# A fused attention + MoE + Sinkhorn-MoE kernel on one core: gate matmuls in column quarters, one reciprocal per set of items, two elementwise steps moved to ScalarE, and weight loads moved in the DMA order

## The chip, the cores and the metric

The kernel runs on one core of a Trainium2 chip. Its engines have an instruction queue each and work through it in order: TensorE (PE in the profile; its weight loads are PEld), VectorE (DVE), ScalarE (ACT), GpSimd (POOL) and SyncE (SP), which issues most of the DMAs. The metric is device time in microseconds of one execution. TensorE's clock has two levels, 1.2 and 2.4 GHz; the profile's PEclk is the mean granted clock of a stretch, 1.00 being 2.4 GHz.

## The reference

```python
# attention: B=4 batches, H=8 heads, S=576 positions, D=64
bias  = -(cum[:, :, :, None] - cum[:, :, None, :])       # cum = cumsum(max(s, 0))
scores = where(causal, -1e9, q @ k.T / 8 + min(bias, 0))
attn  = exp(scores - scores.max(-1)); attn /= attn.sum(-1) + 1e-9
x = (attn @ v) as (2304, 512)
# MoE1: w_in (512, 2048), w_out (2048, 512)
h = x @ w_in;  g = where(h > 0, h, exp(min(h, 0)) - 1);  x = g @ w_out
# MoE2: w_gate (512, 8), w1 (8, 512, 1024), w2 (8, 1024, 512)
P = exp(x @ w_gate - max)
for _ in range(8):
    P /= P.sum(1) + 1e-9;  P /= P.sum(0) + 1e-9;  P *= 2304 / 8
out = sum over e of P[:, e] * (max(x @ w1[e], 0) @ w2[e])
```

All in float32.

## The kernel before, in words

**Order.** The program is written by a small planner: `flow.pe(cost, fn)` writes a piece of TensorE work and advances a model clock, and `flow.after(dt, fn)` writes the work behind it (evictions, softmax steps) once that clock has gone on by dt. The framework then sets the order of each engine's queue; an engine takes its queue strictly in that order.

**Attention.** A job is a pair of heads of one batch; an item is 64 query rows of a job. Batch 0 is cut in two chunks ("A", keys up to 256, four items a job; "B", the other five items), batches 1 to 3 are whole chunks ("F"), four jobs each. Items go in sets (`SETS`), whose scores are made together by `qk_set` (L302). For each item GpSimd makes the bias tile R (`r_step`, L273 and L276); VectorE adds the scores and takes the row's extreme (L321, into `sm`); ScalarE takes the exponential with its row sum (L329, followed by a read of the accumulator); VectorE adds 1e-9 to that sum and takes the reciprocal (L333, L334), an item at a time; GpSimd multiplies R by it (L337, `norm`). TensorE then transposes R (L364, L370), ScalarE and VectorE copy the transposes out, and `pv_piece` multiplies by V (L431). R has five buffers, and a new R waits for the transpose of an old one.

**MoE1.** Its matmuls (L677 for w_in, L709 for w_out, 12 per group) split each float32 into two fp32r parts, so a weight is decoded first: loaded by SyncE into `st` (L581, `w_dma`), then seven operations on VectorE and two on ScalarE (L614 to L634). The activation is `relu` and exp on ScalarE (L685, L686), then on VectorE a combination (L689), the rounding of the result to fp32r (L691) and the remainder (L692). The first groups run between the attention pieces, so the attention of later batches lies beside MoE1 of the earlier ones. `w_dma` is first called after the DMAs of the first attention jobs.

**Gate.** When a batch's MoE1 output `acc` is complete, `gate(b)` multiplies it by w_gate (L789): five blocks of up to 128 tokens, in each the tokens are the stationary operand and the eight columns of w_gate stream past, four 128-row steps of the model width, each float32 matmul in two instructions: 40 for a batch. VectorE copies the result to `P_t` (L797, L799).

**Sinkhorn and MoE2.** After the gate of the last batch the eight Sinkhorn rounds start (`rows` on VectorE, L833 to L837, then `cols` with a matmul with ones, L844, then L848 to L850). They are written between the MoE2 products (L1023; A, B and C in the names) and second layers (L1092, b). From about 750 us to the end MoE2 alone runs.

Of the kernel before, what the change touches and what calls it, by code (L numbers as in the profile page):

```python
# [92 lines left out]
def kernel(  # L93
# [17 lines left out]
    NX = 3  # L111

# [20 lines left out]
    for b in range(B - 1, B - 1 - NX, -1):  # L133
# [17 lines left out]
        "wg": cst.tile([P, 4, E], F32, tag="wg", name="wg"),  # L151
# [128 lines left out]
    sms = {}  # L280

    def qk_set(n):
# [22 lines left out]
        base = set_cost(n) + 0.05  # L305
        for i, c0, keys, ps in later:
            base = softmax(i, c0, keys, ps, base)

    def softmax(i, c0, n, ps, base):
# [4 lines left out]
        if i not in sms:  # L314
            sms[i] = att.tile([P, 8], F32, tag="sm", name=f"sm{i}", bufs=8)
# [10 lines left out]

        def ex():
            mn = sm[:, 2:3] if m == LAST else sm[:, 0:1]
            nc.scalar.activation(R[:, 0:keys], R[:, 0:keys], AF.Exp, scale=-1.0, bias=mn,  # L329
                                 accum_out=sm[:, 3:4])  # L330
# [5 lines left out]
        def norm():  # L336
            nc.gpsimd.tensor_scalar(out=R[:, 0:keys], in0=R[:, 0:keys], scalar1=sm[:, 5:6], scalar2=1.0,  # L337
                                    op0=ALU.mult, op1=ALU.mult)
# [3 lines left out]
        if last:  # L342
            flow.after(base + 0.2 + d, ex)
            flow.after(base + 0.55 + 2 * d, rec)
            flow.after(base + 0.75 + 2 * d, norm)
            ready["t", i] = flow.now + base + 1.15 + 3.2 * d
# [100 lines left out]
    set_chunk = []  # L447
    for j, (k, b, p, part) in enumerate(jobs):
        at = {m: job_items[j][0] + x for x, m in enumerate(spans[part])}
        seen_r = set()  # L450
        for x in SETS[part]:
# [5 lines left out]
            set_chunk.append(k)  # L457
    bundles = []
# [211 lines left out]
    def l1_group(u, k, f, w, c0, n):  # L670
        def fn():
# [29 lines left out]
    def l2_group(u, k, q, d, w, c0, n):  # L701
        def fn():
# [14 lines left out]
            def ev():  # L717
# [9 lines left out]
                if x2[b] == 8:  # L727
                    gates.append(b)
# [48 lines left out]
    def gate(b):  # L777

        x, wg_t = accs[b], phc["wg"]
        ps = ps_s.tile([P, 512], F32, tag="S", name=f"gate{b}")  # L780
        parts, t0 = [], b * S
        while t0 < (b + 1) * S:
            r0 = t0 % P
            n = min(P - r0, (b + 1) * S - t0)
            parts.append((t0 // P, r0, n, t0 - b * S))
            t0 += n
        for i, (tt, r0, n, c0) in enumerate(parts):
            for d in range(4):
                nc.tensor.matmul(ps[r0 : r0 + n, 8 * i : 8 * i + 8], x[:, d, c0 : c0 + n], wg_t[:, d, :],  # L789
                                 start=(d == 0), stop=(d == 3))  # L790
        whole = [i for i, x in enumerate(parts) if x[2] == P]
        half = next(i for i, x in enumerate(parts) if x[2] < P)

        def ev():
            L = phc["P"]
            i, tt = whole[0], parts[whole[0]][0]
            nc.vector.tensor_copy(L[:, tt : tt + 4, :], ps[:, 8 * i : 8 * i + 32].rearrange("p (t e) -> p t e", t=4))  # L797
            tt, r0, n, _ = parts[half]
            nc.vector.tensor_copy(L[r0 : r0 + n, tt, :], ps[r0 : r0 + n, 8 * half : 8 * half + 8])  # L799
            phc["logits"] = phc.get("logits", 0) + 1  # L800
        flow.after(0.2, ev)
# [29 lines left out]
    def rows():  # L831
# [6 lines left out]
        phc["step"] += 1  # L838

# [24 lines left out]
    def extras(force=False):  # L864
        while extra and (force or extra[0][0]()):
# [279 lines left out]
    nc.sync.dma_start(phc["wg"], wg)  # L1145
    nc.vector.memset(ones, 1.0)
    make_identity(nc, ident)
    nc.gpsimd.memset(mask, 0.0)
# [36 lines left out]
    w_dma()  # L1185

    def att_wait():
        t = att_next_ready()
        if t > flow.now:
            flow.flush(t)  # L1190
            flow.now = t

# [14 lines left out]
    for g in range(len(groups)):  # L1207
# [31 lines left out]
        while gates:  # L1239
            flow.pe(2.5, lambda: gate(gates.pop(0)))  # L1240
# [4 lines left out]
    while gates:  # L1245
        flow.pe(2.5, lambda: gate(gates.pop(0)))
# [53 lines left out]
```

## Time and profile before

| | |
|---|---|
| median of three runs | 2211.27 us (2206.74 to 2213.00) |
| the profiled execution | 2213.01 us, of which the span of the profile 2211.2 us |
| TensorE busy | 2151.1 us (97%), 12236 matmuls |
| VectorE, ScalarE, GpSimd busy | 59%, 43%, 37% |
| mean granted clock of TensorE | 0.983 |

The profile is of one execution, and its span leaves out 1.8 us of that execution's time. A TensorE that is busy is not at full speed: its clock may be at the lower level, and short matmuls cost more than their columns. Idle time of an engine, and what ended it, is listed per engine as a wait.

### The profile page before, as it was taken

To read this page: it belongs to the slowest core of one execution; us is meant where nothing else is said; L and a number is where in the kernel's file an instruction comes from. 1 tells how busy PE (TensorE), PEld (TensorE's weight loads), DVE (VectorE), ACT (ScalarE), POOL (GpSimd) and SP (SyncE) were. 2 spreads that over 40 slices of the span, in tenths; PEclk is the share of its full clock that TensorE was granted. 3 is DMA by queue.
4 is the path that set the end of the run, shared out by engine and by line. 5 is a ranking of instruction groups with operands and counts; after the bars stand their busy time and mean duration, and the time that the engine had idled before them with its cause. 6 is when DMAs were issued, how large, how long until landed. Compare 5 with 4: busy or idle time off the path is not lost.

```text
span 2211.2 us, 33504 instructions
## 1 busy us (share of the span) xinstructions
PE 2151.1 (97%) x12236; PEld 1901.1 (86%) x12236; DVE 1294.1 (59%) x2921; ACT 940.2 (43%) x2201; POOL 823.3 (37%) x1046
## 2 busy tenths in 40 slices
PE   6789999999999999999999999999999999999999
PEld 3357988999998898989998989989899899899898
DVE  5678698555756755555555555555555455555554
ACT  3565545343433444344434444343434443443432
POOL 5676343232402343333333343433333333434330
PEclk8899999999999999999999999999999999999999
DMA  6454444243562421222215221222115221222121
GB/s 198 154 167 169 145 169 159 79 131 106 188 229 96 150 77 59 66 77 67 67 58 195 77 77 58 67 68 76 65 60 195 77 70 56 76 67 77 58 67 38
DMA packets 102227, 228.55 MB, mean 103 GB/s; under 512 B 8816, under 2 KB 24688, under 8 KB 102064
## 3 DMA queue, kind: packets, MB, share of 16 engines
q1 hardware_dynamic: 97456, 209.65, 28.9%
q10 hardware_dynamic: 4608, 16.78, 1.9%
q8 instruction: 96, 1.57, 0.3%
q14 instruction: 67, 0.55, 0.1%
HBM read 189.10 MB, written 37.30 MB: 102 GB/s over the span
## 4 chain that ended last, share of the span: by engine, by line
PE 88%; DVE 5%; POOL 2%; DMA 1%; ACT 1%; issue 1%; SPq 0%; POOLq 0%; DVEq 0%; ACTq 0%
PE b L1092 36%; PE A L1023 18%; PE C L1023 9%; PE n L709 7%; PE m L677 7%; PE B L1023 5%; PE S L302 2%; PE X L431 2%; PE T L364 1%; PE gate L789 1%; DVE R L321 1%; POOL R L273 1%; DVE h L692 0%; DMA xr<-x_d 0%; DVE r L689 0%
## 5 line engine op out<-in xcount | busy, mean ns | idle before, releaser
L1092 PE MATMUL b<-w,h 128*128 128x512 f32 x3456 | 844.7, 393 | 0.0
L1092 PEld LDWEIGHTS b<-w,h 128*128 128x128 f32 x3456 | 645.5, 188 | 125.1
L906 POOL TENSOR_TENSOR w1c<-S,w1c 128x512 fp32r<-128x512 f32 x192 | 263.6, 1395 | 860.6 <-ACT w1c L905 860.6
L1023 PE MATMUL A<-xc,w1c 128*128 128x384 f32 x2304 | 449.5, 336 | 0.0
L1106 DVE SCALAR_TENSOR_TENSOR acc<-b,P_t,acc 128x512 f32<-128x512 f32 x264 | 197.5, 748 | 423.1 <-PE b L1092 423.1
L1023 PEld LDWEIGHTS A<-xc,w1c 128*128 128x128 f32 x2304 | 406.3, 188 | 7.8
L1036 ACT ACTIVATE h<-pre_P 128x384 fp32r<-128x384 f32 x288 | 151.4, 526 | 437.6 <-DVE pre_P L1049 437.3
L677 PE MATMUL m<-xT,w 128*128 128x288 f32 (+2 forms) x1536 | 231.3, 305 | 2.9 <-DVE r L689 1.5
L1023 PE MATMUL C<-xc,w1c 128*128 128x384 f32 x1152 | 233.9, 337 | 0.0
L709 PE MATMUL n<-h,w 128*128 128x288 f32 (+2 forms) x1536 | 222.3, 299 | 3.3 <-DVE r L689 1.6
L677 PEld LDWEIGHTS m<-xT,w 128*128 128x128 f32 x1536 | 214.2, 194 | 12.4 <-issue 5.0
L709 PEld LDWEIGHTS n<-h,w 128*128 128x128 f32 x1536 | 207.3, 188 | 17.3 <-issue 11.1
L1023 PEld LDWEIGHTS C<-xc,w1c 128*128 128x128 f32 x1152 | 206.0, 189 | 7.5
L906 DVE TENSOR_TENSOR w<-sw,w 128x512 fp32r<-128x512 f32 x192 | 155.5, 831 | 59.9 <-ACT w L905 59.9
L1039 DVE SCALAR_TENSOR_TENSOR h<-pre_P,h 128x384 fp32r<-128x384 f32 x288 | 160.8, 558 | 12.3 <-ACT h L1036 0.5
L273 POOL TENSOR_SCALAR R<-cum,cum_m 128x256 f32<-128x256 f32 (+4 forms) x144 | 101.8, 707 | 155.5 <-PE T L370 90.6
L337 POOL TENSOR_SCALAR R<-R,sm 128x64 f32<-128x64 f32 (+8 forms) x144 | 92.5, 650 | 118.6 <-DVE sm L334 64.0
L1036 ACT ACTIVATE h<-A 128x384 fp32r<-128x384 f32 x96 | 47.2, 491 | 192.8 <-PE A L1023 192.8
L905 ACT CAST w<-sw 128x512 fp32r<-128x512 f32 x192 | 109.4, 619 | 21.5 <-PE n L709 16.8
L1057 ACT COPY pre_P<-A 128x384 f32<-128x384 f32 x192 | 92.4, 481 | 60.1 <-PE A L1023 60.1
L1023 PE MATMUL B<-xc,w1c 128*128 128x384 f32 x576 | 117.5, 339 | 0.0
L1023 PEld LDWEIGHTS B<-xc,w1c 128*128 128x128 f32 x576 | 104.6, 190 | 7.8 <-issue 0.2
(162 smaller groups left out, 2288.2 us busy)
## 6 DMA issues: line engine op xcount, KB each, us to landing
sw<-in_w_dram SPq DMA_DIRECT2D x192, 512.0 KB, 3.3
w<-w_sc SPq DMA_DIRECT2D x56, 512.0 KB, 3.6
w_sc<-w ACTq DMA_DIRECT2D x32, 512.0 KB, 3.3
xc_d<-xs SPq DMA_DIRECT2D x28, 384.0 KB, 3.2
xc<-xc_d SPq DMA_DIRECT2D x14, 768.0 KB, 6.0
QK<-in_qk_dram SPq DMA_DIRECT2D x16, 576.0 KB, 5.1
st<-in_wi_dram SPq DMA_DIRECT2D x16, 512.0 KB, 4.5
st<-in_wo_dram SPq DMA_DIRECT2D x16, 512.0 KB, 4.0
```

Source lines behind the costliest of these rows:

```text
L273: nc.gpsimd.tensor_scalar(out=t[:, 0:w], in0=ct[j].rearrange("p w k -> p (w k)")[:, S * z : S * z + w], scalar1=8.0, scalar2=cum_m[:, z, m ...
L337: nc.gpsimd.tensor_scalar(out=R[:, 0:keys], in0=R[:, 0:keys], scalar1=sm[:, 5:6], scalar2=1.0, op0=ALU.mult, op1=ALU.mult)
L677: nc.tensor.matmul(ps[:, 0:n], t[:, a, d * P : (d + 1) * P], x[:, z, d, c0 : c0 + n], start=(d == 0 and o == 0), stop=(d == 3 and o == 2))
L709: nc.tensor.matmul(ps[:, 0:n], t[:, a, f * P : (f + 1) * P], h[:, z, c0 : c0 + n], start=(f == 0 and o == 0), stop=(f == 3 and o == 2))
L905: nc.scalar.copy(hi, x)
L906: eng.tensor_tensor(out=lo, in0=x, in1=f32(hi), op=ALU.subtract)
L1023: nc.tensor.matmul(ps, t[:, a, wi_, kt * P : (kt + 1) * P], x[:, z, kt], start=(first and kt == 0 and o == 0), stop=(kt == 1 and o == 2), ...
L1036: nc.scalar.activation(h[:, 0], src, AF.Relu)
L1039: nc.vector.scalar_tensor_tensor(out=h[:, 1], in0=src, scalar=0.0, in1=f32(h)[:, 0], op0=ALU.max, op1=ALU.subtract)
L1057: nc.scalar.copy(new(name), ps)
L1092: nc.tensor.matmul(ps, h[:, z, c0 : c0 + P], t[:, a, :], start=(f == 0 and o == 0), stop=(f == 3 and o == 2))
L1106: nc.vector.scalar_tensor_tensor(out=a, in0=ps, scalar=q, in1=a, op0=ALU.mult, op1=ALU.add)
```

## The change

- **Gate.** `wg` is stored 32 columns wide (24 of them zero). `gate(b, z)` takes a column part z of the batch (256 or 320 tokens): the four 128-row steps are now four matmuls with w_gate stationary and `acc` streaming, each writing its own 32 partitions of one PSUM tile. ScalarE copies the tile out (`lt`), and `gate_sum` adds the four quarters and turns the tokens to partitions, by a matmul of each block of `lt` with a selection matrix `sel`. VectorE copies the logits to `P_t` as before. The queue of gates is a list of such steps, run between MoE1 groups.
- **Softmax.** The row sums of a set stand in one tile (`sums`), and one pair of VectorE operations a set makes all their reciprocals; the multiplications of the set follow. For the chunks A and B (batch 0) they are on ScalarE, for the others on GpSimd as before.
- **MoE1.** The rounding of the activation to fp32r (L691) is on ScalarE.
- **Sinkhorn.** A column step is written no sooner than 3 us of model time after the row step.
- **DMAs.** The first two weights are requested right after the first QK, ahead of the other DMAs of the start; w_gate is requested after those.

```diff
+    SINKGAP = 3.0
+    NORM_ACT = 2
...
+    def norm(i, q):
+        R, keys = Rt[i], 64 * (items[i][1] + 1)
+        if set_chunk[place[i][0]] < NORM_ACT:
+            nc.scalar.activation(R[:, 0:keys], R[:, 0:keys], AF.Copy, scale=q)
+        else:
+            nc.gpsimd.tensor_scalar(out=R[:, 0:keys], in0=R[:, 0:keys], scalar1=q, scalar2=1.0,
+                                    op0=ALU.mult, op1=ALU.mult)
...
         def rec():
-            nc.vector.tensor_scalar(out=sm[:, 4:5], in0=sm[:, 3:4], scalar1=1e-9, scalar2=None, op0=ALU.add)
-            nc.vector.reciprocal(sm[:, 5:6], sm[:, 4:5])
+            nc.vector.tensor_scalar(out=su[:, 0:count], in0=su[:, 0:count], scalar1=1e-9, scalar2=None, op0=ALU.add)
+            nc.vector.reciprocal(su[:, 5 : 5 + count], su[:, 0:count])
+            for t in set_t[n_set]:
+                norm(t, su[:, 5 + place[t][1] : 6 + place[t][1]])
...
-                nc.vector.tensor_copy(h[:, 0, c0 : c0 + n], r[:, 0:n])
+                nc.scalar.copy(h[:, 0, c0 : c0 + n], r[:, 0:n])
...
+    def gate(b, z):
         x, wg_t = accs[b], phc["wg"]
+        cut = [0, 256 + 64 * (b % 2), S]
+        c0, n = cut[z], cut[z + 1] - cut[z]
+        lt = mo1.tile([P, 320], F32, tag="lt", name=f"lt{b}_{z}", bufs=1)
+        ps = ps_s.tile([P, 512], F32, tag="S", name=f"gate{b}_{z}")
+        for d in range(4):
+            nc.tensor.matmul(ps[32 * d : 32 * d + 32, 0:n], wg_t[:, d, :], x[:, d, c0 : c0 + n],
+                             start=True, stop=True)
+        def ev():
+            nc.scalar.copy(lt[:, 0:n], ps[:, 0:n])
+            gates.append((gate_sum, b, z, lt, c0, n))
+        flow.after(1.1, ev)
+
+    def gate_sum(b, z, lt, c0, n):
...
+        for i, (tt, r0, m, at) in enumerate(parts):
+            nc.tensor.matmul(ps[r0 : r0 + m, 8 * i : 8 * i + 8], lt[:, at : at + m], phc["sel"],
+                             start=True, stop=True)
+        if z == 0:
+            gates.append((gate, b, 1))
...
+        phc["due"] = flow.now + SINKGAP
...
-        while extra and (force or extra[0][0]()):
+        while extra and (force or (extra[0][0]() and flow.now >= phc.get("due", 0.0))):
...
     qk_load(0)
-    nc.sync.dma_start(phc["wg"], wg)
+    w_dma()
...
-    w_dma()
+    nc.sync.dma_start(phc["wg"][:, :, 0:E], wg)
+    sel = phc["sel"]
+    nc.gpsimd.tensor_tensor(out=sel, in0=ident[:, 0:E], in1=ident[:, 32 : 32 + E], op=ALU.add)
+    for i in (64, 96):
+        nc.gpsimd.tensor_tensor(out=sel, in0=sel, in1=ident[:, i : i + E], op=ALU.add)
```

The queues of the two programs show what moves. A row is one operation, output `<-` inputs, its shape and how often it stands there in a row; a float32 matmul is one row here and two instructions in the trace.

TensorE's queue from the gate of the last batch to the second transfer of the Sinkhorn's start, before:

```order
L789 MATMUL gate_8314<-wg,acc_7331 64x8 x4
L789 MATMUL gate_8314<-wg,acc_7331 128x8 x7
L1023 MATMUL A_8344<-xc_0_7154,w1c_7565 128x384 x3
L789 MATMUL gate_8314<-wg,acc_7331 128x8 x9
L1023 MATMUL A_8344<-xc_0_7154,w1c_7565 128x384 x3
L1023 MATMUL C_8355<-xc_3_7189,w1c_7565 128x384 x6
L812 MATMUL mxt<-ident,small 1x128
```

and of the change:

```order
L809 MATMUL gate_0_8203<-acc_7220,wg 32x320 x3
L1066 MATMUL A_8233<-xc_0_7041,w1c_7454 128x384
L809 MATMUL gate_0_8203<-acc_7220,wg 32x320
L1066 MATMUL A_8233<-xc_0_7041,w1c_7454 128x384 x4
L827 MATMUL gs_0_8209<-sel,lt_0_8202 64x8
L827 MATMUL gs_0_8209<-sel,lt_0_8202 128x8 x2
L809 MATMUL gate_1_8216<-acc_7220,wg 32x256 x4
L1066 MATMUL A_8233<-xc_0_7041,w1c_7454 128x384
L1066 MATMUL C_8244<-xc_3_7075,w1c_7454 128x384 x2
L827 MATMUL gs_1_8222<-sel,lt_1_8215 128x8 x2
L1066 MATMUL C_8244<-xc_3_7075,w1c_7454 128x384 x4
L854 MATMUL mxt<-ident,small 1x128
```

Twenty gate matmuls have become eight and five (`gs`); before each `gs` stand four or three product matmuls. In the gates of the other batches 24 matmuls of MoE1 stand there.

VectorE's queue at the start, before (cum_m and cum are what the first R is made of):

```order
L247 SCALAR_TENSOR_TENSOR s_raw<-ones,s_raw 32x576
L1167 COPY aB_106<-s_raw 32x9x64
L245 TENSOR_SCALAR cum_134<-cum_134 128x256
L247 SCALAR_TENSOR_TENSOR cum_134<-ones,cum_134 128x256
L1174 TENSOR_SCALAR cum_m<-cT 64x144 x2
```

and of the change (db and da belong to the decoding of the first two weights):

```order
L250 SCALAR_TENSOR_TENSOR s_raw<-ones,s_raw 32x576
L1211 COPY aB_107<-s_raw 32x9x64
L638 TENSOR_SCALAR db_196<-db_196 128x512
L639 TENSOR_SCALAR da_195<-db_196 128x512
L638 TENSOR_SCALAR db_218<-db_218 128x512
L641 SCALAR_TENSOR_TENSOR da_195<-st_114,da_195 128x512
L1218 TENSOR_SCALAR cum_m<-cT 64x144 x2
L248 TENSOR_SCALAR cum_139<-cum_139 128x256
L1221 TENSOR_SCALAR cum_m<-cT 64x144
L250 SCALAR_TENSOR_TENSOR cum_139<-ones,cum_139 128x256
```

Four decoding operations, for which both weights must have landed, now stand ahead of cum_m.

ScalarE's queue at the start, in the change (before, no multiplication stands between the exponentials):

```order
L349 ACTIVATE R_169,sums_184<-R_169,sm_183 128x64
L349 ACTIVATE R_169,sums_184<-R_169,sm_185 128x128
L349 ACTIVATE R_186,sums_207<-R_186,sm_206 128x192
L349 ACTIVATE R_186,sums_207<-R_186,sm_208 128x256
L319 ACTIVATE R_169<-R_169,sums_184 128x64
L319 ACTIVATE R_169<-R_169,sums_184 128x128
L349 ACTIVATE R_209,sums_233<-R_209,sm_232 128x64
L349 ACTIVATE R_209,sums_233<-R_209,sm_234 128x128
```

The rows of L319 are the multiplications; they wait for VectorE's reciprocals, and the next job's exponentials stand behind them.

## Rows read from the trace of the kernel before

**Rows 1.** Windows: stretch, length, busy us (count) of PE, PEld, DVE, ACT, POOL, PEclk, DMA.

```profile
0.00:125.00 125.00, 93.05 (x497) 48.93 (x498) 77.85 (x302) 56.69 (x169) 77.61 (x147) 0.84 0.55 180
125.00:200.00 75.00, 67.83 (x510) 48.04 (x511) 64.10 (x233) 48.52 (x154) 55.92 (x91) 0.98 0.54 180
...
560.00:620.00 60.00, 55.44 (x406) 54.23 (x406) 42.41 (x75) 26.86 (x65) 27.45 (x24) 0.97 0.71 236
...
685.00:750.00 65.00, 57.23 (x277) 51.12 (x276) 46.33 (x111) 26.66 (x56) 28.38 (x29) 0.87 0.42 137
750.00:2211.00 1461.00, 1457.48 (x7279) 1311.96 (x7277) 775.31 (x1290) 593.94 (x1218) 510.58 (x542) 1.00 0.23 77
```

**Rows 2.** Windows, same columns: each of the four gates and the stretch behind it.

```profile
400.50:404.80 4.30, 4.30 (x44) 4.26 (x42) 0.90 (x3) 0.85 (x2) 0.00 (x0) 0.99 0.01 4
404.80:410.00 5.20, 5.20 (x29) 5.20 (x29) 2.33 (x8) 1.08 (x3) 0.00 (x0) 0.68 0.00 0
...
439.80:445.60 5.80, 5.80 (x42) 5.77 (x41) 0.21 (x2) 0.63 (x2) 0.58 (x1) 0.72 0.00 0
445.60:450.00 4.40, 4.40 (x23) 4.40 (x23) 1.99 (x8) 1.71 (x4) 0.69 (x1) 0.60 0.05 7
...
580.80:586.00 5.20, 4.74 (x44) 4.61 (x43) 5.19 (x9) 2.98 (x7) 3.40 (x3) 0.97 0.40 146
586.00:592.00 6.00, 6.00 (x36) 6.00 (x36) 3.99 (x12) 2.97 (x7) 1.35 (x1) 0.74 0.81 269
...
685.80:692.80 7.00, 7.00 (x45) 6.96 (x44) 1.62 (x2) 0.62 (x1) 2.45 (x4) 0.66 0.77 237
692.80:700.00 7.20, 7.20 (x28) 6.55 (x28) 2.25 (x8) 1.84 (x5) 3.00 (x3) 0.62 0.00 1
```

**Rows 3.** Chain that ended last, 600 to 800 us: start, us, what.

```profile
685.89 2.22 PE gate L789 x22
...
689.21 3.64 PE gate L789 x18
```

**Rows 4.** TensorE's waits, 0 to 125 us: us in total, times, longest.

```profile
PE T L364 <- POOL R L337: 11.5, 6, 2.5
...
PE T L370 <- POOL R L337: 2.4, 1, 2.4
```

**Rows 5.** TensorE's waits, 200 to 2211 us, same columns.

```profile
PE col L844 <- DVE small L837: 7.8, 5, 2.9
...
PE n L709 <- DVE r L689: 1.6, 1, 1.6
```

**Rows 6.** TensorE timeline near 460 us: start, us, line, shapes of the first matmul.

```profile
460.59 1.07 PE L302 MATMUL S<-QK 64*64 64x512 f32 x8
```

**Rows 7.** Chain that ended last, 0 to 300 us: one job's V matmuls.

```profile
184.44 2.21 PE X L431 x20
```

**Rows 8.** Groups by line, 0 to 200 us: busy us, mean ns, then idle before.

```profile
L337 POOL TENSOR_SCALAR R<-R,sm 128x64 f32<-128x64 f32 (+8 forms) x70 | 49.0, 705 | 23.8 <-DVE sm L334 10.2 <-DVE aA L378 3.6 <-ACT r L685 2.9
L329 ACT ACTIVATE R<-R,sm 128x64 f32<-128x64 f32 (+8 forms) x71 | 39.6, 559 | 21.5 <-DVE sm L321 15.9 <-DVE sm L325 5.5
...
L618 DVE SCALAR_TENSOR_TENSOR da<-st,da 128x512 int32<-128x512 int32 x16 | 11.6, 723 | 0.0
...
L334 DVE RECIPROCAL sm<-sm 128x1 f32<-128x1 f32 x70 | 10.2, 151 | 0.1
...
L333 DVE TENSOR_SCALAR sm<-sm 128x1 f32<-128x1 f32 x70 | 9.5, 141 | 5.8 <-ACT R L329 5.4
```

**Rows 9.** Timeline of the start: the first R, and one item's two reciprocal operations.

```profile
8.84 0.85 POOL L273 TENSOR_SCALAR R<-cum,cum_m 128x128 f32<-128x128 f32 x2 [6.14 <-DVE cum_m L1174]
...
21.17 0.12 DVE L333 TENSOR_SCALAR sm<-sm 128x1 f32<-128x1 f32 x1
...
25.37 0.15 DVE L334 RECIPROCAL sm<-sm 128x1 f32<-128x1 f32 x1
```

**Rows 10.** Groups by line, VectorE, 200 to 690 us.

```profile
L691 DVE CAST h<-r 128x288 fp32r<-128x288 f32 (+2 forms) x115 | 40.2, 351 | 2.7
```

More of the change, by code (lines that the diff above doesn't have):

```diff
@@ L278, in r_step @@
         cum_advance()
-    sms = {}
+    sms, sums = {}, {}
     def qk_set(n):
@@ L305, in qk_set @@
         base = set_cost(n) + 0.05
+        later.sort(key=lambda x: place[x[0]][1] - 9 * (x[1] > 0))
         for i, c0, keys, ps in later:
             base = softmax(i, c0, keys, ps, base)
+    NORM_FIXED = 0.2
+    def norm(i, q):
[5 more added lines that the diff above has]
+                                    op0=ALU.mult, op1=ALU.mult)
     def softmax(i, c0, n, ps, base):
@@ L325, in ttr @@
                 nc.vector.tensor_tensor(out=sm[:, 2:3], in0=sm[:, 0:1], in1=sm[:, 1:2], op=ALU.min)
+        n_set, at, count = place[i]
+        if last and n_set not in sums:
+            sums[n_set] = att.tile([P, 10], F32, tag="sums", name=f"sums{n_set}", bufs=3)
+        su = sums.get(n_set)
         def ex():
@@ L343, in softmax @@
             flow.after(base + 0.2 + d, ex)
-            flow.after(base + 0.55 + 2 * d, rec)
-            flow.after(base + 0.75 + 2 * d, norm)
-            ready["t", i] = flow.now + base + 1.15 + 3.2 * d
+            if at == count - 1:
+                flow.after(base + 0.55 + 2 * d, rec)
+                when = flow.now + base + 0.95 + 2 * d
+                for t in set_t[n_set]:
+                    when += NORM_FIXED + 64 * (items[t][1] + 1) / 800.0
+                    ready["t", t] = when
         return base + 0.1 + n / 950.0
@@ L457 @@
             set_chunk.append(k)
+            for x, t in enumerate(set_t[-1]):
+                place[t] = (len(sets) - 1, x, len(set_t[-1]))
     bundles = []
@@ L727, in ev @@
                 if x2[b] == 8:
-                    gates.append(b)
+                    gates.append((gate, b, 0))
             flow.after(12 * _mm(n) + 0.05, ev)
@@ new lines, in gate_sum @@
+    def gate_sum(b, z, lt, c0, n):
+        ps = ps_s.tile([P, 512], F32, tag="S", name=f"gs{b}_{z}")
+        parts, t0 = [], b * S + c0
+        while t0 < b * S + c0 + n:
+            r0 = t0 % P
+            m = min(P - r0, b * S + c0 + n - t0)
+            parts.append((t0 // P, r0, m, t0 - b * S - c0))
+            t0 += m
+        for i, (tt, r0, m, at) in enumerate(parts):
[3 more added lines that the diff above has]
+            gates.append((gate, b, 1))
@@ L791, in gate @@
         whole = [i for i, x in enumerate(parts) if x[2] == P]
-        half = next(i for i, x in enumerate(parts) if x[2] < P)
+        half = [i for i, x in enumerate(parts) if x[2] < P]
         def ev():
             L = phc["P"]
[L796 to L800, printed above, removed]
@@ L801, in gate @@
-        flow.after(0.2, ev)
+            i, tt, k = whole[0], parts[whole[0]][0], len(whole)
+            nc.vector.tensor_copy(L[:, tt : tt + k, :],
+                                  ps[:, 8 * i : 8 * i + 8 * k].rearrange("p (t e) -> p t e", t=k))
+            for i in half:
+                tt, r0, m, _ = parts[i]
+                nc.vector.tensor_copy(L[r0 : r0 + m, tt, :], ps[r0 : r0 + m, 8 * i : 8 * i + 8])
+            phc["logits"] = phc.get("logits", 0) + z
+        flow.after(0.8, ev)
@@ L1191, in att_wait, with gates_run @@
             flow.now = t
+    def gates_run():
+        while gates:
+            fn, *args = gates.pop(0)
+            flow.pe(1.0, lambda: fn(*args))
     def att_end(k):
@@ L1238 @@
                 w1_prep(int(g > m2["w"] + 24), 0.0)
-        while gates:
-            flow.pe(2.5, lambda: gate(gates.pop(0)))
+        gates_run()
         w_advance(g)
@@ L1245 @@
     while gates:
-        flow.pe(2.5, lambda: gate(gates.pop(0)))
+        gates_run()
+        flow.drain()
     pools["xp%d" % ((B - 1) % NX)].release()
```

24 lines of the change are left out of this document (6 added, 18 removed).

## Prediction

> **What bounds the kernel now.** I read the windows by stage first, because 97% busy over the span hides where the rest lies. From 750 us to the end TensorE is busy 1457.48 of 1461 us at a clock of 1.00 [rows 1]; no edit touches that stage, so it ends as much earlier as it starts. Up to 750 us the loss is in four places: 32 us of idle time and a clock of 0.84 in the first 125 us, 7.2 us idle to 200 us, 4.6 us between 560 and 620 us, 7.8 us and a clock of 0.87 between 685 and 750 us [rows 1]. The second thing to see is that the gates are costly though TensorE is never idle in them. Each takes 4 to 6 us, and three of the four stretches right behind a gate run at a granted clock of 0.60 to 0.68, the fourth at 0.74, so most of each at 1.2 GHz; in the first gate itself it is still 0.99, at 2.4 GHz [rows 2]. Third, the waits: in the first 125 us TensorE's largest wait is for GpSimd's multiplication by the reciprocal, 11.5 and 2.4 us [rows 4]; behind 200 us it is the Sinkhorn column step that waits for VectorE, 7.8 us in five waits [rows 5].
>
> **The gates: -17 us.** Before, the four take 4.30, 5.80, 5.20 and (2.22 + 3.64) 5.86 us, together 21.2 [rows 2, 3]. The new first half streams 576 columns a batch through four quarters, two instructions each: 576 x 4 x 2 = 4608 column passes. Nothing in the trace streams through quarters of the array's columns. The nearest rows: the V matmuls use halves of the columns, and one job's 20 instructions carry 4 x 1216 = 4864 passes in 2.21 us, 0.454 ns a pass [rows 7]; the score matmuls use 64 x 64 corners, all four in turn, and the set of the 512- and 448-key pieces carries 4 x 960 = 3840 passes in 1.07 us, 0.279 ns [rows 6]. So more tiles side by side cost less per pass. At 0.279 a batch costs 1.3 us, at 0.454 it costs 2.1, and if quarters don't overlap at all, while the halves do, twice that, 4.2. I take 1.3, as four tiles are what the score matmuls have too. The second half is five matmuls a batch of the old kind (weights of 128 columns, eight columns streamed), 10 instructions at 4.30 / 40 = 0.107 us [rows 2]: 1.1 us. That is 2.4 us a batch, 9.6 in all: -11.6.
>
> The clock comes on top. Behind the gates it costs 5.2 x 0.32 + 4.4 x 0.40 + 6.0 x 0.26 + 7.2 x 0.38 = 7.7 us [rows 2]. In place of 40 short matmuls in a row stand at most 10, and full groups of MoE1 between them; I expect the three dips in MoE1 to go (5.0 us) and half of the last (1.4): -6.4.
>
> Against it, the last gate has little cover. In the queues four product matmuls stand between its first part and the `gs` that needs ScalarE's copy, three between its second part and its `gs`; the copy is bounded by ScalarE's other operations of that size, about 0.56 us [rows 8], and a queued weight rounding can stand ahead of it. I charge 1.5 us for both waits and the longer way to the Sinkhorn start (0 to 4). For the other batches 24 matmuls cover the copy. Sum -16.5, rounded to -17; bounds -20 (nothing for the waits, all dips gone) and -2 (quarters one after the other: 21.2 against 21, clock -6, wait +4).
>
> The Trainium skill, "TensorE: Matmul & The Clock Gate", section "Measured speedup vs the span model", gives 3.07 times for four packed tiles, not four. By it the 4.2 us of a batch would be an estimated 1.4 instead of 1.3, so the sum would be 0.4 us worse; no run here shows it yet.
>
> **The softmax of batch 0 and the early weights: -8 us.** GpSimd's multiplications cost it 705 ns each [rows 8], and in its queue stand new R tiles, which wait for transposes; so the multiplications wait for work they don't need. In the first two chunks 36 of them (16 + 20) go to ScalarE. Its exponentials of the same shapes cost 559 ns [rows 8], which I take as the price: 20 us more on an engine that is busy 56.7 of 125 us [rows 1], so 61%: it has room. TensorE's 13.9 us of waits [rows 4] don't all vanish, since ScalarE has its own queue (copies, exponentials, decoding): I take half, -7. The clock in that stretch costs up to 125 x 0.16 = 20 us [rows 1], but much of that lies where TensorE has nothing to do; I take -3. Against it stands the start. The first R is made at 8.84 us, when cum_m is there [rows 9]. Now cum_m stands behind four decoding operations, at most 0.72 us each [rows 8], and these behind two weight transfers. Before, no decoding stood ahead of it, so the first R comes later: +2 (0 to 3). The same decoding is then missing later, where it held a reciprocal back from 21.17 to 25.37 us [rows 9]; that is in the -7. Sum -8. Bounds: -22 (all of the waits, 10 us of clock, no delay) and +8 (the waits come back behind ScalarE's queue and the start is later).
>
> The reciprocal pair costs 151 + 141 ns [rows 8] and there are 56 pairs now for 144: VectorE loses 26 us of work. In batches 1 to 3 the first item of a set now waits for the last one's exponential, up to four more of 559 ns. TensorE has MoE1 groups meanwhile, and loses 7 us in all up to 200 us [rows 1]: I put 0, between -4 and +4.
>
> **The rounding on ScalarE: -2 us.** VectorE gives away 128 roundings of 351 ns [rows 10], 45 us. That pays only where TensorE waits for it: in the 4.6 us of idle time between 560 and 620 us, where VectorE is busy 42 of 60 us [rows 1], and in single waits such as 1.6 us [rows 5]. The path gets one more hand-over between engines, covered by the four PSUM buffers of MoE1 (`ps_m`). I take -2 (-6 to +3). What moves to ScalarE (about 50 us by the same 559 ns less the short shapes) finds it less than half busy.
>
> **The Sinkhorn: -2 us.** Between the first and the last column step TensorE's queue has 102 product and 50 second-layer matmuls before, 89 and 60 after: about the same work. So the gap of 3 us evens the spacing but adds little cover; VectorE's chain stays as it is. The last step, ahead of which stood 12 + 4 matmuls, now has 9 + 12. Of 7.8 us [rows 5] I take back 2; bounds -7.8, and +3 if the later start pushes the last step into the second layers that need it.
>
> **Sum.** 2213.0 (the execution profiled, span 2211.2 and 1.8 around it) - 17 - 8 - 2 - 2 = 2184. The median of the runs before is 1.7 below that execution, so I forecast **2182**.
>
> **Rivals.**
> *Start won whole.* If GpSimd's queue was the only brake of batch 0, TensorE's waits all go and the clock follows: -20 instead of -8, 2170. For it: GpSimd is the releaser of the largest wait [rows 4]. Against: VectorE is as busy as GpSimd there, 77.85 and 77.61 us [rows 1]. Chance 0.18.
> *Waits change their name.* ScalarE takes the multiplications in order, behind four exponentials and the copies of transposes, and the waits stay as long: start 0, so 2190. Chance 0.16.
> *Quarters don't run side by side.* Then the gates give about 5 us instead of 17: 2194. For it: no row shows quarters. Against: [rows 6] against [rows 7]. Chance 0.14.
> *ScalarE is blocked: slower.* A multiplication at the head of ScalarE's queue waits for the set's reciprocal, which waits in VectorE's queue, once for 4.2 us behind decoding [rows 9]; the next job's exponentials, the copies of transposes and the MoE1 activations stand behind it. Batch 0 has 20 sets. The other edits give 21 us; so the kernel is slower by 6.6 us from 27.6 us on, 1.4 us a set beyond what the waits before cost; at 2 us a set it ends at 2230. Against: early decoding empties VectorE's queue. Chance 0.04.
> The Trainium skill, "ScalarE: Activation LUTs", section "Rules for kernel authors", would have multiplications on VectorE and not on ScalarE: it is on this rival's side. Whether the trace agrees is open, since no row before has a plain multiplication on ScalarE.
>
> **How the numbers follow.** About 6.6 us (0.3%) is what a measurement of this kernel tells from no change. The forecast's case, 2172 to 2192, has 0.43; the first three rivals 0.48; the slow one 0.04; 0.05 is for two of the bad cases together (start at +8 and gates at -3: 2200 to 2214). Faster is all of the first two groups: 0.90; same 0.06; slower 0.04. The range takes in the 2194 of the quarters and reaches to 2201 for part of the mixed case, and below to 2164, where the start gives all and the Sinkhorn its waits; some 0.15 is left out.
>
> **What would show it.** The gates' `gate` matmuls take 0.5 to 0.8 us a part, and the clock behind them is 1.00. TensorE's waits for GpSimd in the first 125 us are gone, those for ScalarE's multiplication are below 7 us; the first R comes at 10 to 12 us. The idle time of 560 to 620 us falls below 3 us; the column steps' waits are 5 to 6 us. The stage behind them takes the same 1461 us. The prediction is wrong if the dips of the clock stay (+6), if a part of the gate takes over 1.5 us, or if batch 0's attention ends later than before.

## The result and the profile after

The changed kernel takes 2188.89 us (median of four executions, 2187.69 to 2194.79), beside 2211.26 for the kernel before: a ratio of 0.9907, 95% interval 0.9884 to 0.9931, so 20.6 us less by the ratio. The profiled execution took 2194.79 us, with a span of 2192.7, 18.2 us less than the profiled execution of before. This one and a second profiled one (2193.68 us) are slower than the other three (2187.69 to 2189.91), so a mark read from their traces can be some 5 us late.

The windows by stage, with the columns of [rows 1]:

```profile
0.00:125.00 125.00, 90.14 (x531) 49.15 (x532) 74.92 (x269) 75.77 (x223) 60.37 (x128) 0.90 0.55 181
125.00:200.00 75.00, 67.97 (x486) 48.57 (x485) 59.31 (x181) 48.67 (x151) 51.20 (x79) 0.96 0.52 179
560.00:620.00 60.00, 53.71 (x368) 49.96 (x367) 35.45 (x63) 31.91 (x81) 23.78 (x21) 0.94 0.70 232
685.00:750.00 65.00, 59.30 (x299) 52.42 (x299) 53.19 (x125) 35.20 (x74) 29.66 (x28) 0.95 0.45 150
750.00:2192.00 1442.00, 1438.99 (x7222) 1307.64 (x7221) 768.46 (x1276) 585.96 (x1201) 509.91 (x540) 1.00 0.23 77
```

The first 125 us did not get better: TensorE is idle 34.9 us there, 3 more than in [rows 1], at a better clock. The stretch from 560 to 620 us is worse (6.3 us idle for 4.6), the one from 685 to 750 better. Where the waits of [rows 4] went shows in TensorE's waits, 0 to 125 us (us in total, times, longest). Before, the score matmuls waited so:

```profile
PE S L302 <- DVE sm L321: 5.8, 4, 3.5
PE S L302 <- DMA QK<-in_qk_dram: 4.5, 1, 4.5
```

and changed:

```profile
PE S L305 <- DVE sm L336: 11.8, 7, 6.9
PE S L305 <- DMA QK<-in_qk_dram: 11.4, 2, 7.0
PE T L385 <- ACT R L319: 3.0, 3, 1.6
```

The multiplication is waited for 3.0 us now (13.9 in [rows 4]), 10.9 less. The score matmuls wait 6.0 us more for VectorE and 6.9 more for the QK transfer. From 200 us on, answering to [rows 5]:

```profile
PE col L887 <- DVE small L879: 4.5, 3, 2.2
PE n L732 <- ACT h L714: 2.7, 1, 2.7
...
PE gs L827 <- ACT lt L813: 0.4, 1, 0.4
```

The gate of batch 0 in TensorE's timeline (start, us, line, shape of the first matmul):

```profile
403.05 0.64 PE L809 MATMUL gate<-acc,wg 128*32 128x256 f32 x8
403.61 3.46 PE L700 MATMUL m<-xT,w 128*128 128x288 f32 x24
406.91 0.51 PE L827 MATMUL gs<-sel,lt 128*128 128x8 f32 x4
407.34 0.75 PE L809 MATMUL gate<-acc,wg 128*32 128x320 f32 x8
408.02 3.45 PE L700 MATMUL m<-xT,w 128*128 128x288 f32 x24
```

The next matmul starts 0.56 and 0.68 us after the two parts, 1.24 in this batch; the forecast was 1.3 by [rows 6]. In batch 2 the order cuts a part into six instructions and two, so that one quarter stands alone in the timeline:

```profile
574.25 0.62 PE L809 MATMUL gate<-acc,wg 128*32 128x256 f32 x2 [0.81 <-DVE acc L744]
574.80 1.84 PE L700 MATMUL m<-xT,w 128*128 128x288 f32 x12
```

One quarter of 256 columns takes 0.55 us to the next matmul, four take 0.56: side by side they cost what one costs, which is 3.9 times. The Trainium skill, "TensorE: Matmul & The Clock Gate", section "Measured speedup vs the span model", has 3.07 times for four tiles along the rows of the array. By that figure a batch was an estimated 1.4 us; the trace of these quarters, which lie along the columns, is better. The timeline also shows the price of cutting a part: both pieces take nearly the time of the whole, so batches 2 and 3, where a part is cut, take 1.86 and 1.89 us for their quarters.

The stretches behind the four gates, with the columns of [rows 2], now run at a clock of 1.00, where they had 0.60 to 0.74. In batch 2's gate itself (572.60 to 587.50 us), where TensorE is idle for 3 us, this execution has 0.89; in the second profiled execution the clock is 1.00 there too.

```profile
412.20:420.00 7.80, 7.80 (x62) 6.52 (x62) 5.27 (x19) 4.90 (x17) 4.12 (x10) 1.00 0.30 81
...
446.50:452.00 5.50, 5.50 (x43) 5.41 (x44) 3.34 (x11) 4.06 (x13) 0.00 (x0) 1.00 0.50 156
...
572.60:587.50 14.90, 11.90 (x78) 9.65 (x76) 11.17 (x19) 9.11 (x22) 5.50 (x6) 0.89 0.63 211
587.50:594.00 6.50, 6.50 (x50) 6.42 (x49) 4.94 (x11) 5.16 (x14) 2.62 (x3) 1.00 0.69 245
...
688.00:694.00 6.00, 6.00 (x36) 5.68 (x35) 3.17 (x7) 3.90 (x9) 3.69 (x3) 1.00 0.28 90
```

The table sets marks of TensorE's timeline side by side, for all runs (us; "end" is the start of the last second-layer matmul; the ratio is to the kernel before, timed beside it, with its 95% interval; a single execution has none). It is read down a column: what an edit gives up to the first gate, up to the last one, and to the end.

| kernel | first R | first V matmul | first gate | last gate | end | ratio |
|---|---|---|---|---|---|---|
| before | 8.84 | 21.37 | 400.65 | 685.83 | 2207.09 | |
| before, again | 8.91 | 21.43 | 400.16 | 686.73 | 2206.30 | |
| before, padded | 8.87 | 21.40 | 404.93 | 692.36 | 2203.89 | 0.9962 (0.9942 to 0.9982) |
| changed | 12.07 | 24.76 | 403.05 | 682.24 | 2188.60 | 0.9907 (0.9884 to 0.9931) |
| changed, again | 11.92 | 24.62 | 405.20 | 682.10 | 2187.47 | |
| tiles moved | 12.01 | 24.72 | 401.66 | 679.74 | 2182.90 | 0.9888 (0.9868 to 0.9908) |
| old gate | 11.98 | 24.66 | 402.67 | 686.41 | 2191.76 | 0.9946 (0.9931 to 0.9961) |
| late weights | 8.82 | 23.00 | 396.75 | 674.45 | 2179.48 | 0.9903 (0.9886 to 0.9920) |
| multiplication on GpSimd | 11.93 | 29.00 | 406.08 | 682.86 | 2187.80 | 0.9928 (0.9915 to 0.9942) |
| rounding on VectorE | 11.93 | 24.61 | 401.67 | 680.20 | 2185.12 | 0.9916 (0.9897 to 0.9935) |
| reciprocal per item | 12.04 | 25.17 | 394.22 | 670.86 | 2175.58 | 0.9848 (0.9830 to 0.9866) |
| no gap | 11.67 | 24.35 | 402.13 | 679.76 | 2187.97 | 0.9930 (0.9915 to 0.9945) |
| late weights, tiles moved | 8.90 | 22.84 | 398.89 | 676.75 | 2178.42 | 0.9883 (0.9865 to 0.9901) |
| the same, batch 1 on ScalarE | 8.80 | 22.98 | 402.28 | 680.55 | 2180.49 | 0.9881 (0.9864 to 0.9899) |

Two things stand out in the rows of before and changed. The first gate does not come earlier but 2.4 to 5.0 us *later*, and both kernels have done the same TensorE work up to there (1392 matmul instructions of MoE1, 512 of scores, 300 transposes, 336 with V). The runs "tiles moved", "old gate" and "no gap" have the changed kernel's instructions up to this mark; with them it lies between 401.66 and 405.20 us, 1.0 to 5.0 later than before. The padded kernel, with the instructions of before, has it at 404.93, so such a mark moves by 4 us without an edit, and the sign is not sure; that no 8 us were gained is. And from the start of the last gate to the end, where the prediction put some 5 us, the kernel gains 13 to 16 us.

### The profile page after: what moved, and what is told of

Same layout as the page of the kernel before. It is cut to its first block, busy times and chain, and to the rows that moved or that the text cites. A ratio compares the mean times of both kernels' runs of the same rounds, so it can differ in the third digit from the quotient of the medians.

```text
span 2192.7 us, 33164 instructions
## 1 busy us (share of the span) xinstructions
PE 2129.9 (97%) x12180; PEld 1892.3 (86%) x12180; DVE 1243.7 (57%) x2621; ACT 1000.9 (46%) x2373; POOL 804.0 (37%) x1014
## 4 chain that ended last, share of the span: by engine, by line
PE 89%; DVE 3%; DMA 3%; POOL 2%; ACT 1%; issue 1%; SPq 0%; POOLq 0%; ACTq 0%; DVEq 0%
PE b L1135 36%; PE A L1066 18%; PE C L1066 9%; PE m L700 8%; PE n L732 7%; PE B L1066 5%; PE S L305 3%; PE X L452 2%; PE T L385 1%; DMA xr<-x_d 1%; POOL R L276 1%; POOL R L279 1%; DMA xc_d<-xs 0%; DVE xc L949 0%; DMA QK<-in_qk_dram 0%
## 5 line engine op out<-in xcount | busy, mean ns | idle before, releaser
L1135 PE MATMUL b<-w,h 128*128 128x512 f32 x3456 | 831.5, 390 | 0.0
L1082 DVE SCALAR_TENSOR_TENSOR h<-pre_P,h 128x384 fp32r<-128x384 f32 x288 | 161.5, 561 | 11.6
L948 ACT CAST w1c<-S 128x512 fp32r<-128x512 f32 x192 | 110.4, 628 | 4.1 <-POOL S L981 3.8
L1100 ACT COPY pre_P<-C 128x384 f32<-128x384 f32 x96 | 46.3, 482 | 143.0 <-PE C L1066 142.8
```

Of the source, the lines that this page charges most:

```text
L948: nc.scalar.copy(hi, x)
L1082: nc.vector.scalar_tensor_tensor(out=h[:, 1], in0=src, scalar=0.0, in1=f32(h)[:, 0], op0=ALU.max, op1=ALU.subtract)
L1100: nc.scalar.copy(new(name), ps)
L1135: nc.tensor.matmul(ps, h[:, z, c0 : c0 + P], t[:, a, :], start=(f == 0 and o == 0), stop=(f == 3 and o == 2))
```

## The experiments

**Is the MoE2 stage faster by its addresses?** First both kernels once more, without an edit:

> The kernel before, profiled once more. Question: the stage of MoE2 behind the last column step became about 7 us shorter in the profile after, though no edit is in it. There two second-layer matmuls in a row start 230.6 ns apart before and 226.7 after, two product matmuls 173.7 before and 175.3 after. Theory of the addresses (the wider gate table and the new table shift the tiles that were allocated behind them by 416 bytes, and with that a matmul's pace): the same 230.6 and 173.7 again. Rival, the pace differs from execution to execution: it moves by a nanosecond or more between executions of this same kernel, towards 226.7. Time 2205 to 2214 by both.

> The changed kernel, profiled once more, as a control for the spread between executions. Theory of the addresses: second-layer matmuls start 226.7 ns apart again, product matmuls 175.3. Rival, the pace differs from execution to execution: other values. The profiled execution of 2194.79 us was the slowest of four of this kernel, so both expect a time of 2187 to 2195.

The mean spacing repeated to 0.1 ns: second-layer matmuls 230.6 ns apart in both executions of before and 226.7 in both of the changed kernel, product matmuls 173.7 and 175.3. ("Matmul" here and in the expectations is one instruction of the trace.) One turn of the repeating order in TensorE's timeline, from its first line to the same place in the next turn, before:

```profile
1001.55 2.93 PE L1092 MATMUL b<-w,h 128*128 128x512 f32 x12
...
1017.15 2.93 PE L1092 MATMUL b<-w,h 128*128 128x512 f32 x12
```

and changed:

```profile
1004.71 2.88 PE L1135 MATMUL b<-w,h 128*128 128x512 f32 x12
...
1020.23 2.88 PE L1135 MATMUL b<-w,h 128*128 128x512 f32 x12
```

The times were 2212.19 and 2193.68 us. So the pace belongs to the kernel and not to the execution. Then the addresses alone:

```diff
 "wg": cst.tile([P, 4, E], F32, tag="wg", name="wg"),
+"pad": cst.tile([P, 104], F32, tag="pad", name="pad"),
```

> The kernel before with one unused tile of 416 bytes a partition behind the gate table, so that every tile allocated behind it lies where it lies in the changed kernel; nothing else differs. Theory of the addresses: second-layer matmuls 226.7 ns apart and product matmuls 175.3, the stage behind the last column step about 7 us shorter, time 2211 - 7 = 2204 us, ratio 0.997. Rival (the pace comes from the execution, or from the time at which the stage begins, and not from addresses): 230.6 and 173.7 as before, 2211 us, ratio 1.000.

Groups by line, TensorE, 760 to 2180 us (busy us, mean ns of one): before,

```profile
L1092 PE MATMUL b<-w,h 128*128 128x512 f32 x3276 | 799.5, 393 | 0.0
L1023 PE MATMUL A<-xc,w1c 128*128 128x384 f32 x2184 | 423.6, 335 | 0.0
```

before with the pad,

```profile
L1093 PE MATMUL b<-w,h 128*128 128x512 f32 x3297 | 791.7, 389 | 0.0
L1024 PE MATMUL A<-xc,w1c 128*128 128x384 f32 x2197 | 429.5, 336 | 0.0
```

and changed:

```profile
L1135 PE MATMUL b<-w,h 128*128 128x512 f32 x3310 | 794.5, 389 | 0.0
L1066 PE MATMUL A<-xc,w1c 128*128 128x384 f32 x2186 | 427.5, 336 | 0.0
```

A tile that nothing uses gives the old kernel the new kernel's pace. From its first second-layer matmul behind the last column step to its last one it takes 1454.8 us, where before takes 1462.2: 7.4 us less, and 8.4 by the ratio. The theory of the addresses is shown; what about the address does it is not.

```diff
-"sel": cst.tile([P, E], F32, tag="sel", name="sel"),
+phc["sel"] = mo1.tile([P, E], F32, tag="sel", name="sel")
```

> The changed kernel with the table that sums the quarters (32 bytes a partition) moved from the pool of constants into that of MoE1, so that the weight and activation tiles of MoE2 lie 384 bytes (a multiple of 64) behind their place of before in place of 416; the instructions are the same. Theory that the place within 64 bytes sets the pace: second-layer matmuls 230.6 ns apart again, time 2189 + 7 = 2196 us, ratio to before 0.993. Rival (another cause): 226.7 stays, 2189 us, ratio 0.990.

The stage came out faster again, not slower (groups by line, as above):

```profile
L1135 PE MATMUL b<-w,h 128*128 128x512 f32 x3333 | 802.3, 390 | 0.0
L1066 PE MATMUL A<-xc,w1c 128*128 128x384 f32 x2178 | 422.1, 334 | 0.0
```

One turn, 36 second-layer and 42 product instructions (the later expectation, which says 12 and 24, counts wrong), takes 15.60 us before, 15.52 changed and padded, 15.48 here. So my sub-theory (the place within 64 bytes) falls: a shift by a multiple of 64 has a pace of its own.

**The gates.**

```diff
-        for d in range(4):
-            nc.tensor.matmul(ps[32 * d : 32 * d + 32, 0:n], wg_t[:, d, :], x[:, d, c0 : c0 + n],
-                             start=True, stop=True)
...
+        for i, (tt, r0, n, c0) in enumerate(parts):
+            for d in range(4):
+                nc.tensor.matmul(ps[r0 : r0 + n, 8 * i : 8 * i + 8], x[:, d, c0 : c0 + n], wg_t[:, d, 0:E],
+                                 start=(d == 0), stop=(d == 3))
```

> The changed kernel with the gate of before (40 matmuls of the row form a batch, no copy to ScalarE, no summing matmul); the tables keep their sizes, so that all tiles stay where they are. Theory of the prediction (the gates give 17 us): four gates of 4.3 to 5.9 us again, a granted clock of 0.6 to 0.75 behind each, time 2189 + 17 = 2206 us, ratio to before 0.998. Rival (what the matmul spacing of MoE2 gives, 7 us, and the other edits make up most of the gain, the gates less than half of it): 2189 + 8 = 2197 us, ratio 0.994.

The ratio lies between the two, nearer to the rival: the gates give 0.0039 of 2211 us, 8.6, half of what was forecast. Where the time goes, from 150 us to the start of the Sinkhorn (time from each matmul's start to the next one's, without idle time, summed by kind from the trace; us):

```
                        before  old gate  changed  changed, again
gate and its sum         19.94     18.84    11.35           10.95
MoE1, two layers        415.95    414.59   413.40          411.06
idle                     14.04     13.29    16.28           17.39
```

The shorter gate saves 7.5 to 7.9 us, MoE1's matmuls run 1.2 to 3.5 us faster, and TensorE is idle 3.0 to 4.1 us more. The old gate stands here for one execution; in the second one of before it sums to 17.84 us and in the padded kernel to 20.72, so the saving is known to about 2 us. At the full clock MoE1's 288-column matmuls are 132.5 ns apart with the old gate as with the new, so what they gain is the clock. By place, the gain is between the first gate and the third (175.85 us with the old gate, 169.76 and 169.70 with the new); from the last gate to the end the old gate takes 1505.35 us and the new one 1506.36 and 1505.37, so the last gate gave nothing. That idle time is in the stretch of batch 2's gate. TensorE's waits, 560 to 620 us, with the old gate:

```profile
PE gate L814 <- DVE acc L744: 2.0, 2, 1.2
PE m L700 <- DVE acc L744: 0.6, 2, 0.4
```

and changed:

```profile
PE m L700 <- DVE acc L744: 2.4, 3, 1.8
PE m L700 <- DVE r L712: 1.8, 1, 1.8
PE m L700 <- ACT acc L742: 0.8, 2, 0.7
```

MoE1 waits there for VectorE and ScalarE either way; as I read it, the long gate was work that filled part of the wait.

**The first weights.**

```diff
     qk_load(0)
-    w_dma()
...
+    w_dma()
     nc.sync.dma_start(phc["wg"][:, :, 0:E], wg)
```

> The changed kernel with the first two expert weights loaded and decoded at the place of before, behind the first set of R. Theory (the early transfers and decodings are what makes the start late: first R at 12.07 us for 8.84, second QK transfer issued at 9.88 us for 4.96): first R at 9 us again, first V matmuls at 21 us for 24.8, and about 3 us less, 2186 us, ratio 0.989. Rival (TensorE makes it up by 125 us anyway, or the decodings then hold the reciprocals back as in the kernel before): the first R at 9 us, but the first gate of batch 0 where it was (403 to 405 us), time 2189 to 2192 us, ratio 0.990 to 0.992.

The first R is back at 8.82 us, the first V matmul at 23.00. The profiled execution gains 6.3 to 8.5 us up to the first gate and keeps it to the end, more than either expected; but at 2185.55 us it is among the shortest of its six, which reach from 2185.42 to 2195.12, and the ratio says 0.9 us. So no gain of the early weights shows; that they cost something, one trace suggests and the times don't settle.

**The multiplication on ScalarE.**

```diff
-    NORM_ACT = 2
+    NORM_ACT = 0
```

> The changed kernel with all multiplications by the reciprocal on GpSimd, as before; the shared reciprocals stay. Theory of the prediction (GpSimd's queue is the brake of batch 0): TensorE waits for the multiplication 10 us or more in the first 125 us again, chunk B's last V matmuls at 119 us for 112, time 2189 + 6 = 2195 us, ratio 0.993. Rival (the waits only change their name; TensorE waited for VectorE and for transfers in the changed kernel, 23 us in the first 125): time 2187 to 2190 us, ratio 0.989 to 0.991.

TensorE's waits, 0 to 125 us:

```profile
PE T L385 <- POOL R L321: 13.7, 6, 3.3
PE S L305 <- DVE sm L336: 9.3, 8, 6.7
PE S L305 <- DMA QK<-in_qk_dram: 4.9, 2, 4.5
```

GpSimd is waited for again, and the transfer 6.5 us less: in sum TensorE is idle 35.6 us for 34.9, the last gate and the end stand where they were. That is on the rival's side (waits change their name). The marks that the theory named came, too: chunk B's last V matmuls start at 117.90 us for 112.16 and 111.55, and the median is 2195.00 us; by the ratio it is 4.6 us longer, with intervals that overlap. Executions of the changed kernel differ by 7 us among themselves (2187.69 to 2194.79), so one end in the same place decides nothing. Up to 5 us are open.

**The rounding.**

```diff
-                nc.scalar.copy(h[:, 0, c0 : c0 + n], r[:, 0:n])
+                nc.vector.tensor_copy(h[:, 0, c0 : c0 + n], r[:, 0:n])
```

> The changed kernel with the rounding of MoE1's inner values back on VectorE (a copy of up to 512 columns, 351 ns each in the profile before). Theory of the prediction (VectorE is the brake of single stretches): the idle time between 560 and 620 us stays at or above 6.3 us, TensorE waits for VectorE in more places before 685 us, time 2189 + 2 = 2191 us, ratio 0.992. Rival (neither engine is waited for there, since the idle time of that stretch did not fall with the edit: 4.6 us before, 6.3 after): time 2187 to 2190 us, the same waits; if ScalarE's extra work is what made the stretch worse, the idle time falls to 4.6 us and the time to 2187 us.

The ratio is 2.0 us above that of the changed kernel, inside its interval, and the trace ends 2.4 to 3.5 us earlier. The idle time of 560 to 620 us is 6.9 us, so neither engine's rounding made it. What the rounding is worth stays open.

**The shared reciprocals.**

```diff
-            nc.vector.reciprocal(su[:, 5 : 5 + count], su[:, 0:count])
-            for t in set_t[n_set]:
-                norm(t, su[:, 5 + place[t][1] : 6 + place[t][1]])
+            nc.vector.reciprocal(su[:, 5 + at : 6 + at], su[:, at : at + 1])
+            norm(i, su[:, 5 + at : 6 + at])
...
-            if at == count - 1:
-                flow.after(base + 0.55 + 2 * d, rec)
...
+            flow.after(base + 0.55 + 2 * d, rec)
+            ready["t", i] = flow.now + base + 1.15 + 3.2 * d
```

> The changed kernel with a reciprocal and a multiplication by itself for each score row block, as before (144 pairs of short VectorE operations for 56); the multiplications of batch 0 stay on ScalarE. Theory (the pairs cost VectorE some 26 us, and the start waits for VectorE, 11.8 us in the first 125): 2 to 4 us slower, 2191 to 2193 us, ratio 0.991 to 0.992. Rival (a set's first rows are ready earlier by up to four exponentials, which is worth as much as the pairs cost): 2187 to 2190 us, ratio 0.989 to 0.991.

Both were wrong by sign or size: 2178.14 us, 13.0 us *less* than the changed kernel by the ratio. The windows, 0 to 125 us:

```profile
0.00:125.00 125.00, 96.94 (x608) 55.36 (x609) 83.88 (x347) 84.35 (x248) 71.00 (x142) 0.97 0.56 185
```

VectorE is busy 9 us longer than in the changed kernel, and TensorE 6.8 us longer at 0.97 for 0.90. TensorE's timeline at the wait of 7 us, changed:

```profile
36.78 1.32 PE L305 MATMUL S<-QK 64*64 64x320 f32 x2 [6.98 <-DMA QK<-in_qk_dram]
38.04 1.55 PE L452 MATMUL X<-aA,V 128*64 128x256 f32 x8
```

and with a reciprocal per item:

```profile
31.57 1.76 PE L305 MATMUL S<-QK 64*64 64x192 f32 x8
...
33.69 0.87 PE L447 MATMUL X<-aA,V 128*64 128x256 f32 x8
...
35.78 1.51 PE L305 MATMUL S<-QK 64*64 64x320 f32 x12 [0.18 <-DMA QK<-in_qk_dram]
```

The transfer lands 1 us apart in the two. With the shared reciprocal the second job's V matmuls (`X`) stand behind the score matmul that waits for it; per item they and other scores stand ahead of it, and the wait is filled. In ScalarE's timeline of the same time, changed,

```profile
33.00 0.66 ACT L637 ACTIVATE db<-st 128x512 f32<-128x512 f32 x1 [3.59 <-DMA st<-in_wi_dram]
33.57 0.62 ACT L319 ACTIVATE R<-R,sums 128x64 f32<-128x64 f32 x2
...
34.54 0.40 ACT L401 COPY aA<-T 128x128 f32<-128x128 f32 x2
```

and per item:

```profile
31.65 0.64 ACT L319 ACTIVATE R<-R,sums 128x64 f32<-128x64 f32 x2 [1.09 <-DVE sums L354]
...
32.79 0.41 ACT L396 COPY aA<-T 128x128 f32<-128x128 f32 x2
33.63 0.68 ACT L632 ACTIVATE db<-st 128x512 f32<-128x512 f32 x1 [0.43 <-DMA st<-in_wi_dram]
```

With a set's multiplications written together, they and the copies of the transposes that the V matmuls need stand behind a decoding (`db`) that waits 3.59 us for its transfer; per item they stand ahead of it. Chunk A's last V matmuls start at 63.36 us changed and at 50.39 per item. The edit moves the reciprocals and, by the `ready` times, the planner's places for the transposes; which of the two counts for more was not tried.

**The gap between Sinkhorn steps.**

```diff
-    SINKGAP = 3.0
+    SINKGAP = 0.0
```

> The changed kernel without the gap of 3 us between Sinkhorn steps. Theory of the prediction (the gap gives 2 us): the waits of the column steps 7 to 8 us for 4.5 to 4.9, time 2189 + 2 = 2191 us, ratio 0.992. Rival (the matmuls ahead of the column steps are the same work in another place): the waits move, the last column step ends at the same time after the first, within 1 us, and the time is 2187 to 2190 us, ratio 0.989 to 0.991.

The column steps wait 6.0 us for 4.5 and 4.9. The last one starts 39.4 us after the first, for 40.7 and 39.7 in the two executions of the changed kernel; with the gap, the work from the last column step to the end takes 1451.1 us for 1454.3. So some 3 us of work are moved ahead of the last step, and less than that is paid there. The trace ends where the changed kernel's does, but this execution was 2.3 to 2.5 us ahead of it at the first column step. From that step to the end it takes 1493.6 us; the seven executions with the gap and the same MoE2 pace (two of the changed kernel; old gate, late weights, multiplication on GpSimd, rounding on VectorE, reciprocal per item) take 1490.5 to 1491.8. So the gap saves 1.8 to 3.1 us by the traces, as the theory has it. The times say 5.1 us, with intervals that overlap.

**Two combinations.** Late weights with moved tiles, and with `NORM_ACT = 4` on top:

> The changed kernel with the first two weights at the place of before (as in the run with late weights) and the table that sums the quarters moved into MoE1's pool (as in the run with moved tiles). Theory (the two are independent: the first gives 2 us or more at the start, the second 2.9 us by the spacing of 15.48 us for 12 second-layer and 24 product matmuls for 15.52): 2184 us, ratio 0.987 to 0.988. Rival (the times of these kernels lie within their spread of 6 to 10 us between executions, and the start's gain is given back up to 685 us): 2187 us, ratio 0.989 to 0.990.

> The kernel with late weights and moved tiles, and the multiplications of batch 1's two chunks on ScalarE too (76 of them in all for 36 now, if batch 1 has as many pieces). TensorE waits 6.6 to 7.4 us for GpSimd's multiplication between 125 and 200 us, in two or three waits of up to 4.1. Theory (GpSimd's queue is the brake there as in batch 0): these waits go, 4 to 6 us less than with late weights and moved tiles alone, about 2179 us, ratio 0.985. Rival (MoE1's work on ScalarE stands in the way of the multiplications, or the waits take another name): the same time as without it, within 2 us, or slower.

The first gave 2184.43 us, the time that the theory expected, but its ratio is only 1.1 us below that of the moved tiles alone: the late weights add little in the times. The second gave the same, 2184.35. TensorE's waits of the second, 125 to 200 us:

```profile
PE S L305 <- DVE sm L336: 4.7, 3, 2.5
PE T L385 <- DVE xT L457: 1.9, 1, 1.9
PE n L732 <- DVE r L712: 1.8, 1, 1.8
```

The 6.6 us of waits for GpSimd are gone, and VectorE is waited for in their place.

The best kernel of all is the changed one with a reciprocal per item, 2178.14 us: 13 us below the change and 33.6 below before (ratio 0.9848). With moved tiles or late weights on top it was not run.

## Why the prediction came out right, point by point

The time (2188.89 for 2182, inside the range) and its side were right, but that it came so near is in part luck: the gates gave half and the start gave nothing, and 8 us of MoE2 that I had at 0 stand in for them.

- **Gates, -17: the mechanism was right, the size was twice too large.** The quarters run side by side, and the clock behind every gate is 1.00. Of the term, the gates' own matmuls were put at -11.6 and measured -7.5 to -7.9. The trace has the old gates at 17.8 to 20.7 us without their waits, where I took 21.2. The new gate takes 2.7 to 2.8 us a batch for 2.4: the quarters 1.6 for 1.3, by the parts that are cut in two, and the summing matmuls 1.2 to 1.3 for 1.1. The clock was put at -6.4: TensorE's mean clock from 200 to 750 us rose from 0.97 to 0.98 and 0.99, but MoE1's matmuls gained only 1.2 to 3.5 us from it, beside the old gate. The waits were put at 1.5, in the last gate; they are 3.0 to 4.1, at batch 2's, which I had as covered by 24 matmuls. What is saved in that gate goes into MoE1's waits; at the last gate, where I had 3.4, nothing was saved to the end.
- **Start, -8: it did not come, by one step.** My own sign of a failure did not show: batch 0's last V matmuls start at 112.16 and 111.55 us, before at 119.24 and 118.47. But less of MoE1 was done meanwhile (70 MoE1 instructions by 125 us, before 81), and the first gate, with the same work behind it, comes 2.4 to 5.0 us later. So attention that ends earlier was no measure of time gained. The step that failed is the shared reciprocal: "In batches 1 to 3 the first item of a set now waits for the last one's exponential ... I put 0", and for batch 0 I counted only what VectorE saves. By the ratios it cost 13 us, with intervals that lie apart. With a reciprocal per item the first gate comes 5.9 to 6.4 us earlier than before, in one execution: for what else touches the start, -8 was about right. The later first R, +2, measured +3.2. (The lower bound, all of the waits and 10 us of clock with no delay, sums to -24 and not to -22.)
- The rival in which *waits change their name* is half borne out: GpSimd's multiplication is gone from the waits, and in its place TensorE waits longer for VectorE (11.8 us for 5.8) and for a transfer (11.4 for 4.5). In the *blocked ScalarE* I had the queue right and the head of it wrong: multiplications and copies stand behind a waiting decoding, and TensorE's V matmuls behind waiting scores. *Quarters not side by side* is out: four take 0.56 us where one alone takes 0.55. The Trainium skill's rule to multiply on VectorE ("ScalarE: Activation LUTs", "Rules for kernel authors") is neither borne out nor refuted: no run here has the multiplication on VectorE.
- **Rounding, -2:** not resolved. The idle time of 560 to 620 us grew to 6.3 us where I expected under 3; the new gate does that, since with the old gate and the rounding on ScalarE it is 2.6. That does not credit the rounding either: the padded kernel, which has it on VectorE, has 2.9.
- **Sinkhorn, -2: about right.** The waits fell from 7.8 to 4.5 us, below the 5 to 6 expected (6.0 without the gap), and from the first column step to the end the gap saves 1.8 to 3.1 us by the traces.
- **MoE2, 0: wrong.** That "no edit touches that stage" is true of its instructions and not of its operands' addresses: -7.4 us by the trace, -8.4 by the ratio.

By the ratios the parts give -8.6 (gates), +13.0 (shared reciprocals), +0.9 (early weights), -4.6, -2.0 and -5.1 (multiplication, rounding, gap, each with overlapping intervals) and -8.4 (addresses), -14.8 together. The whole is -20.6. By the two intervals together each difference is uncertain by 4 to 6 us, so the rest of 5.8 us is not assigned. One edit was not tried by itself: the changed kernel sorts the score pieces of a set before their softmax (`later.sort`), and every run of it does.

## What to carry to other kernels

Joining small operations of several items saves their engine time and delays the first item; where in-order queues stand behind it, read what each queue then holds at its next wait, since that can cost more than the engine time gives. Compare two kernels at a mark up to which both have done the same work: one chain that ends earlier can be paid for by the work beside it. Before an edit is credited with a faster stage, give the old kernel the new one's addresses with an unused tile: that alone was worth 0.4% here. And a slow piece that stands where TensorE would wait is worth less than its length.

## What the hardware showed

The spacing of matmuls in a row in MoE2 depends on where the tiles that were allocated behind a table of constants lie in SBUF, the on-chip memory of the operands, and repeats in each profiled execution. Second layers (512 columns) are 230.6 ns apart before, 226.7 with all those tiles 416 bytes further, 226.8 with 384; products (384 columns) 173.7, 175.3 and 173.5, all at a granted clock of 1.00. Four gate quarters along the columns of the array take 0.56 us for 256 columns, one alone 0.55. ScalarE rounds MoE1's tiles (288 columns and two other shapes, 115 of them) in 432 ns in the mean, 49.6 us in all, VectorE in 351 [rows 10]; its multiplications took 555 ns each (36, 18.3 us), as the 559 taken from its exponentials [rows 8].
